# A two-layer MLP on one Trainium2 core: `x @ w_in` of three passes written as Strassen's seven half-size products

## The chip, the cores and the metric

The kernel runs on one core of a Trainium2 chip. Its engines are TensorE (PE; PEld is its weight load), VectorE (DVE), ScalarE (ACT), GpSimd (POOL) and SyncE (SP), which here only issues DMA transfers. The metric is the device time of one execution in microseconds (us); the median of three runs is given.

## The reference

An attention block produces `x` (2304 tokens by 512), and two MLP layers follow, each with `d_ff` = 2048:

```
x = attention(q, k, v)                      # 2304 x 512
h = x @ moe_w_in;   g = h * sigmoid(h);     x2  = g @ moe_w_out
h = x2 @ moe2_w_in; g = elu(h);             out = g @ moe2_w_out
```

All inputs are float64 or float32 and the result is float32. Weights come as float64 bit patterns and are decoded to float32 on the chip.

## The kernel before

Each matrix product is done in fp32r (32-bit matmul operands) with every operand split into a high and a low part; three of the four products of parts are kept: high x high, high x low, low x high. So one 128-wide contraction step costs three matmuls.

The MLP part has four passes: (layer, half of `d_ff`) = (0, 0), (0, 1), (1, 0), (1, 1). A pass holds the split weights of 8 slices `f` of 128 hidden units and runs over the tokens in blocks: nine blocks of 256 in the first pass, which runs beside the attention, and one block of 256 and four of 512 in each later pass. A unit is one block and one `f`. `g1` (L510) does `x @ w_in` of a unit: 4 contraction steps x 3 = 12 matmuls into a PSUM tile `ph`. ACT, DVE and POOL then make the activation and its split (`t`, `gh`, `gl`, L527 to L539; layer 0: tanh, add and multiply; layer 1: minimum, exp, add and maximum). `g2` (L574 for layer 0, L576 for layer 1), issued 3 units later (`LAG`), multiplies by `w_out` and sums over the 8 `f` in PSUM. In layer 0 the moving operand of `g2` is `g` (so a matmul is as wide as the token block), in layer 1 it is the weight (always 512 wide). The first half's sums go to DRAM (`yp`) and come back as `part` in the second half, where they are added (L591, L597).

The weights of the next pass are loaded (L139, L144, three staging buffers `ws`), decoded (`wf`: two ACT steps L158, L160 and three DVE steps L169, L170, L176) and split (`wh` on ACT L186, `wl` on POOL or DVE L188) a step at a time between the matmuls: `tick`, called four times in every `g1` and `g2`, takes one step of a list. Every engine executes its instructions in the order in which the program issues them; there is one SP queue for nearly all transfers. `x32` holds the attention's result, later `x2`, in SBUF for the whole run; `split_x` (L471, L474) splits it again for every block of every pass.

## Time and profile before

| quantity | value |
|---|---|
| three timed runs | 967.91, 968.86, 969.98 us (median 968.86) |
| profiled execution, first to last instruction (span) | 966.0 us |
| PE busy / DVE busy / ACT busy / POOL busy | 928.7 / 512.0 / 438.5 / 352.9 us |
| mean granted TensorE clock | 0.980 of full speed |

The page states only a span for the profiled execution and no total of its own; the median of the timed runs is 2.9 us above that span. Sums below are made against the span, and those 2.9 us are then put on top. The first 272 us hold the attention together with first-pass blocks, 272 to about 375 us the rest of the first pass, and the three later passes fill the time from about 375 us to 962 us. Since matmuls are pipelined and their ends are modelled, the busy time of PE says only that matmuls were in flight; the step between the starts of two matmuls is what one costs.

### The profile page before, as it was taken

What the parts mean: (1) busy time and instruction counts of PE and PEld (TensorE: products, weight loads), DVE (VectorE), ACT (ScalarE), POOL (GpSimd) and SP (SyncE); (2) the same over time, 40 slices, a digit from 0 to 9 for tenths busy, and PEclk for the clock granted to TensorE, in tenths of its full rate; (3) what the DMA queues carried; (4) which work ended last, traced back from release to release, by engine and by line L of the source; (5) the groups of instructions that cost most, each with busy time, mean ns of one, the idle gap of its engine ahead of it and who ended that gap; (6) DMA issues with size and microseconds to landing.
All of it is one profiled execution on the core that took longest, in us unless ns stands there. A gap on an engine that the chain in (4) does not pass through costs nothing.

```text
span 966.0 us, 16438 instructions
## 1 busy us (share of the span) xinstructions
PE 928.7 (96%) x6488; PEld 800.9 (83%) x6493; DVE 512.0 (53%) x841; ACT 438.5 (45%) x995; POOL 352.9 (37%) x363
## 2 busy tenths in 40 slices
PE   8388989999999999999999999999999999999998
PEld 5267879999999999888888887888888888888886
DVE  6677544444537857545453367656543544334232
ACT  4676545455446666443433445434333433222221
POOL 4577543553443354222223432222224422222221
PEclk9679999999999999999999999999999999999999
DMA  9944343233233632322121103122101011112021
GB/s 184 217 151 110 86 111 87 71 92 81 53 102 123 191 125 89 108 66 77 55 91 42 43 23 97 57 88 66 44 1 43 27 40 66 44 44 88 1 87 44
DMA packets 93485, 77.61 MB, mean 80 GB/s; under 512 B 61664, under 2 KB 82144, under 8 KB 92384
## 3 DMA queue, kind: packets, MB, share of 16 engines
q1 hardware_dynamic: 91008, 75.97, 26.9%
q8 instruction: 51, 0.84, 0.4%
q10 hardware_dynamic: 2400, 0.59, 0.3%
q14 instruction: 26, 0.21, 0.1%
HBM read 62.39 MB, written 14.16 MB: 79 GB/s over the span
## 4 chain that ended last, share of the span: by engine, by line
PE 62%; DVE 1%; ACT 1%; issue 0%; DMA 0%; SPq 0%; DVEq 0%; ACTq 0%
PE ph L510 31%; PE y L576 19%; PE y L574 12%; DMA ws<-in_moe_w_out_dram 0%; DVE part L597 0%; DVE xl L474 0%; DVE t L532 0%; ACT t L533 0%; ACT xh L471 0%; DVE wf L176 0%; DVE wf L169 0%; ACT gh L537 0%; DVE wf L170 0%; ACT ws L160 0%; ACT wf L158 0%
## 5 line engine op out<-in xcount | busy, mean ns | idle before, releaser
L539 POOL TENSOR_TENSOR gl<-t,gh 128x256 fp32r<-128x256 f32 (+1 forms) x192 | 204.5, 1066 | 526.2 <-ACT gh L537 472.8
L510 PE MATMUL ph<-xh,wh 128*128 128x256 f32 (+1 forms) x768 | 251.6, 340 | 4.7 <-DVE t L529 2.4
L510 PE MATMUL ph<-xl,wh 128*128 128x256 f32 (+1 forms) x768 | 250.4, 339 | 3.4 <-DVE xl L474 3.3
L510 PE MATMUL ph<-xh,wl 128*128 128x256 f32 (+1 forms) x768 | 177.9, 337 | 0.0
L510 PEld LDWEIGHTS ph<-xh,wh 128*128 128x128 f32 x768 | 145.6, 190 | 22.9 <-DVE t L529 3.0
L510 PEld LDWEIGHTS ph<-xl,wh 128*128 128x128 f32 x768 | 145.6, 190 | 21.2 <-DVE xl L474 5.0
L537 ACT CAST gh<-t 128x256 fp32r<-128x256 f32 (+1 forms) x192 | 98.8, 514 | 115.9 <-DVE t L529 63.4
L574 PE MATMUL y<-gh,wh 128*128 128x256 f32 (+1 forms) x448 | 145.3, 324 | 0.0
L510 PEld LDWEIGHTS ph<-xh,wl 128*128 128x128 f32 x768 | 127.9, 189 | 15.6 <-issue 0.6
L574 PE MATMUL y<-gl,wh 128*128 128x256 f32 (+1 forms) x448 | 140.6, 314 | 0.0
L574 PE MATMUL y<-gh,wl 128*128 128x256 f32 (+1 forms) x448 | 140.6, 314 | 0.0
L533 ACT ACTIVATE t<-t 128x512 f32<-128x512 f32 (+1 forms) x80 | 47.1, 589 | 195.8 <-DVE t L532 195.8
L529 DVE SCALAR_TENSOR_TENSOR t<-t,ph 128x256 f32<-128x256 f32 (+1 forms) x112 | 55.3, 494 | 143.6 <-ACT t L527 143.5
L532 DVE TENSOR_SCALAR t<-ph 128x512 f32<-128x512 f32 (+1 forms) x80 | 51.0, 637 | 122.3 <-PE ph L510 121.9
L576 PE MATMUL y<-wh,gh 128*128 128x512 f32 x288 | 112.2, 390 | 0.0
L576 PE MATMUL y<-wh,gl 128*128 128x512 f32 x288 | 112.2, 390 | 0.0
L576 PE MATMUL y<-wl,gh 128*128 128x512 f32 x288 | 112.0, 389 | 0.0
L527 ACT ACTIVATE t<-ph 128x256 f32<-128x256 f32 (+1 forms) x112 | 49.7, 444 | 121.9 <-PE ph L510 115.8
L474 DVE TENSOR_TENSOR xl<-x,xh 128x256 fp32r<-128x256 f32 (+1 forms) x96 | 68.4, 730 | 45.7 <-ACT xh L471 45.1
L574 PEld LDWEIGHTS y<-gh,wh 128*128 128x128 f32 x448 | 85.6, 191 | 7.4 <-issue 1.0
L574 PEld LDWEIGHTS y<-gl,wh 128*128 128x128 f32 x448 | 85.7, 191 | 5.0
L574 PEld LDWEIGHTS y<-gh,wl 128*128 128x128 f32 x448 | 85.5, 191 | 5.0
(90 smaller groups left out, 1207.8 us busy)
## 6 DMA issues: line engine op xcount, KB each, us to landing
ws<-in_moe_w_in_dram SPq DMA_DIRECT2D x32, 512.0 KB
ws<-in_moe_w_out_dram SPq DMA_DIRECT2D x32, 512.0 KB
rows<-in_v_dram SPq DMA_DIRECT2D x36, 144.0 KB
yp<-yo SPq DMA_DIRECT2D x10, 512.0 KB
part<-yp SPq DMA_DIRECT2D x10, 512.0 KB
out_dram<-part SPq DMA_DIRECT2D x18, 256.0 KB
yp<-yo SPq DMA_DIRECT2D x4, 1024.0 KB
part<-yp SPq DMA_DIRECT2D x4, 1024.0 KB
```

The source lines that it names most:

```text
L474: nc.vector.tensor_tensor(lo[c - 1], src[:, c - 1, :], hi[c - 1].bitcast(F32), ALU.subtract)
L510: nc.tensor.matmul(ph[:, :nb], a[:, c, :], b[c], start=m == 0, stop=m == 3 * KC - 1)
L527: nc.scalar.activation(t, h, AF.Tanh, scale=0.5)
L529: nc.vector.scalar_tensor_tensor(t, t, 1.0, h, op0=ALU.add, op1=ALU.mult)
L532: nc.vector.tensor_scalar_min(t, h, 0.0)
L533: nc.scalar.activation(t, t, AF.Exp)
L537: nc.scalar.copy(gh, t)
L539: nc.gpsimd.tensor_tensor(gl, t, gh.bitcast(F32), ALU.subtract)
L574: nc.tensor.matmul(y[d // share][:, h:h + nb], wm[:, sl], gm, start=first and d % share == 0, stop=last, skip_group_check=True)
L576: nc.tensor.matmul(y[d], gm[:, sl], wm, start=first, stop=last)
```

## The change

The first pass keeps its form (nine blocks of 256). In the three later passes the tokens are taken as three duos of 2 x 384 (768) tokens, and `x @ w_in` of a duo is done with Strassen's scheme (in Winograd's form): tokens, contraction (2 x 256) and hidden units (pairs of slices `f`, index `j` = 0 to 3) are each halved, and seven products of half-size blocks replace eight. A product is 4 `j` x 2 contraction steps x 3 = 24 matmuls, 384 wide (L944). Products 0, 2, 3 and 4 add up in one set of four PSUM banks, 1, 5 and 6 in the other. After products 0, 2 and 3 ACT copies the running sums out (L956); after 1, 5 and 6 DVE adds such a copy to a bank (L952). Only then does the next product of the set continue in the bank.

The half-size operands are sums: of weights (four DVE additions per pair, L761 to L767), and of `x` (four DVE additions of 128x768 per duo, L803). Each operand is split again (ACT cast L733; subtraction on DVE L736 or POOL L735). `g2` follows for each half of the duo: 8 slices, 384 wide in layer 0 (L1033), 512 wide in layer 1 (L1035). `x` no longer stays in SBUF: when the attention is done, four transfers write it to DRAM (`xd`), and each duo's part is loaded back (`xraw`); between the layers it goes through DRAM too (`x2`).

The work of ACT, DVE, POOL is no longer taken a step at a time. Each piece is a `Job` with an engine, an assumed duration, predecessors, an event of PE after which it may start, and a due time. `pump` is called after each product step (or quarter of a `g2` slice); it issues, among the jobs that could start before the planner's present time, the one with the earliest start, and of equals the one due first. `need` issues at once what the next matmuls depend on. Subtractions may go to POOL or DVE, whichever the planner expects to be done first; DVE jobs with `port=True` and all POOL jobs are planned one after the other.

On PE a stretch of the second layer reads so before: the last matmuls of a `g2` on the 512 hidden-side columns (`y`), then a `g1` unit of 12 (`ph`), then `g2` again.

```order
L576 MATMUL y_7509<-wh_7090,gh 128x512
L576 MATMUL y_7509<-wh_7090,gl 128x512
L576 MATMUL y_7509<-wl_7091,gh 128x512
L510 MATMUL ph<-xh,wh_6780 128x512
L510 MATMUL ph<-xl,wh_6780 128x512
L510 MATMUL ph<-xh,wh_6780 128x512
L510 MATMUL ph<-xl,wh_6780 128x512
L510 MATMUL ph<-xh,wh_6780 128x512
L510 MATMUL ph<-xl,wh_6780 128x512
```

Now the second layer has runs of product matmuls; here the end of product 1 and the start of product 2 (`wAA`, `wSS`: weight sums; `xhr`, `xlr`: split sums of `x`; `pc`: the banks).

```order
L944 MATMUL pc_8908<-xhr_5102,wAA3h_5091 128x384
L944 MATMUL pc_8908<-xlr_5103,wAA3h_5091 128x384
L944 MATMUL pc_8908<-xhr_5102,wAA3l_5092 128x384
L944 MATMUL pc_8836<-xhr_5412,wSS0h_5094 128x384
L944 MATMUL pc_8836<-xlr_5413,wSS0h_5094 128x384
L944 MATMUL pc_8836<-xhr_5412,wSS0l_5095 128x384
L944 MATMUL pc_8836<-xhr_5412,wSS0h_5094 128x384
L944 MATMUL pc_8836<-xlr_5413,wSS0h_5094 128x384
```

The alternation of `g1` and `g2` is gone: 28 such steps of six 384-wide matmuls stand together, then 16 slices of `g2`.

On ACT in the second layer the old order repeats exponentials (L533) and casts (L537) of units with steps of the decoder (`wf`, `ws`) and casts of `x` between them.

```order
L160 ACTIVATE ws_7392<-ws_7392 128x512
L533 ACTIVATE t_7587<-t_7587 128x512
L537 CAST gh_7588<-t_7587 128x512
L158 ACTIVATE wf_7606<-ws_7454 128x512
L160 ACTIVATE ws_7454<-ws_7454 128x512
L533 ACTIVATE t_7628<-t_7628 128x512
L537 CAST gh_7629<-t_7628 128x512
L471 CAST xh_7655<-x32_98 128x512
L471 CAST xh_7662<-x32_98 128x512
```

Now, between products 0 and 4 of the first duo of the last pass, the copies of the running sums (`hg` from `pc`, L956) stand in one queue with decoding (`raw`, `ws`), casts and activations.

```order
L704 ACTIVATE raw3_4396<-ws_8786 128x512
L705 ACTIVATE ws_8786<-ws_8786 128x512
L956 COPY hg0_4408<-pc_8836 128x384
L956 COPY hg1_4409<-pc_8846 128x384
L956 COPY hg2_4410<-pc_8855 128x384
L704 ACTIVATE raw4_4397<-ws_8794 128x512
L705 ACTIVATE ws_8794<-ws_8794 128x512
L956 COPY hg3_4411<-pc_8866 128x384
L733 CAST xhr_5100<-xt_4405 128x768
L841 ACTIVATE hg0_4408<-pc_8879 128x384
L733 CAST wh1_5536<-raw3_4396 128x512
L844 ACTIVATE hg0_4408<-hg0_4408 128x384
```

The copies of product 0 are queued around two decoder steps (`ws_8794`) that need a transfer to have landed; product 2 on those banks waits for each copy.

On DVE at the end of the first pass, after the attention, decoding is now mixed with the first sums of `x` and of weights (`xraw`: `x` loaded back from DRAM; `s1t`: a weight sum; `t`: activations of first-pass units).

```order
L762 TENSOR_TENSOR raw1_4394<-raw0_4393,raw1_4394 128x256
L516 SCALAR_TENSOR_TENSOR t_4600<-t_4600,ph_4585 128x256
L474 TENSOR_TENSOR xl_4617<-x32_98,xh_4610 128x256 x2
L717 SCALAR_TENSOR_TENSOR raw2_4395<-ws_4386,raw2_4395 128x512
L803 TENSOR_TENSOR xt_4405<-xraw3_4404,xraw1_4402 128x768
L516 SCALAR_TENSOR_TENSOR t_4646<-t_4646,ph_4630 128x256
L709 TENSOR_SCALAR raw3_4396<-raw3_4396 128x512
L803 TENSOR_TENSOR xraw1_4402<-xraw1_4402,xraw0_4401 128x768
```

Before, only decoder steps, `xl` and evictions stood between those activations (L529 then, L516 now); L803 waits for the transfers of `xraw`, and the next activation is queued behind it.

The diff, cut to its core:

```diff
-    WIDE = [(0, 2 * P)] + [(t_, 4 * P) for t_ in range(2 * P, NT, 4 * P)]
-    BLOCKS = {(0, 0): [(t_, 2 * P) for t_ in range(0, NT, 2 * P)], (0, 1): WIDE, (1, 0): WIDE, (1, 1): WIDE}
     NB0 = 2 * P
-    NBM = 4 * P
+    BLOCKS = [(t_, NB0) for t_ in range(0, NT, NB0)]
+    NB = 3 * P
+    NDUO = NT // (2 * NB)
+    PASSES = [(0, 1), (1, 0), (1, 1)]
...
+    ON_ACT = (0, 2, 3)
+    T_TICK, T_C, T_G = 0.52, 1.04, 2.08
+    PASS = NDUO * (7 * FP // 2 * T_C + 2 * FP * T_G)
...
-    def following(u):
-        layer, ps, n, _ = u
-        if n + 1 < len(BLOCKS[layer, ps]):
-            return layer, ps, n + 1
-        if ps + 1 < NPASS:
-            return layer, ps + 1, 0
-        return (layer + 1, 0, 0) if layer == 0 else None
-
-    ypart = {}
-
-    units = [
-        (layer, ps, n, f) for layer in range(2) for ps in range(NPASS)
-        for n in range(len(BLOCKS[layer, ps])) for f in range(FP)
-    ]
+    held = {}
+
+    units = [(n, f) for n in range(len(BLOCKS)) for f in range(FP)]
...
+    def keep_x(b):
+
+        xd[b] = dram.tile([P, KC, S], F32, tag=f"xd{b}", name=f"xd{b}")
+        nc.sync.dma_start(xd[b], x32[:, :, b * S:(b + 1) * S])
...
+        def start(self):
+
+            if self.gate is not None and self.gate not in events:
+                return None
+            t = events.get(self.gate, -1e9)
+            if self.port:
+                t = max(t, clock_of["port"])
+            for p in self.preds:
+                if p.end is None:
+                    return None
+                t = max(t, p.end)
...
+        def emit(self):
+            t = self.start()
+            assert t is not None
+            waiting.remove(self)
+            self.fn()
+            clock_of[self.eng] = t + self.dur
+            if self.port:
+                clock_of["port"] = t + self.dur
+            self.end = t + self.dur + self.lat
+
+    def pump(t):
+
+        while True:
+            best = None
+            for job in waiting:
+                s = job.start()
+                if s is not None and s < t and (best is None or (s, job.due) < best[:2]):
+                    best = (s, job.due, job)
+            if best is None:
+                return
+            best[2].emit()
...
+    ACT_ = {2 * P: 0.41, NB: 0.50, DM: 0.62, 2 * NB: 0.82}
+    VEC_ = {2 * P: 0.42, NB: 0.56, DM: 0.69, 2 * NB: 0.96}
+    GPS_ = {2 * P: 0.74, NB: 1.02, DM: 1.30, 2 * NB: 1.86}
...
+    def two_jobs(hi, lo, src, width, preds, gate, due):
+
+        a = Job("A", ACT_[width], lambda: nc.scalar.copy(hi(), src), preds, gate)
+        return Job(
+            "G", GPS_[width], lambda: nc.gpsimd.tensor_tensor(lo(), src, hi().bitcast(F32), ALU.subtract), [a], due=due,
+            other=("V", VEC_[width], lambda: nc.vector.tensor_tensor(lo(), src, hi().bitcast(F32), ALU.subtract)),
+        )
...
+            s0 = Job("V", VEC_[H], lambda s=s, o=o: sub(s, o[:, :H], o[:, H:], ALU.add), [do] + before.get(j - 2, []), port=True)
+            s1_ = Job("V", VEC_[H], lambda e=e, o=o: sub(o[:, :H], e[:, :H], o[:, :H], ALU.subtract), [s0, de], port=True)
+            aa = pair("AA", e, DM, [de], 0)
+            sa = pair("SA", o, DM, [s1_], 3 * NJ * T_C)
+            st = pair("S1", s, H, [s0], 5 * NJ * T_C)
+            m0 = Job("V", VEC_[H], lambda e=e, s=s: sub(e[:, :H], s, e[:, :H], ALU.subtract), [aa, s1_], port=True)
+            m1 = Job("V", VEC_[H], lambda e=e: sub(e[:, H:], e[:, H:], e[:, :H], ALU.subtract), [m0], port=True)
+            ss = pair("SS", e, DM, [m1], 2 * NJ * T_C)
+            before[j] = [st, m0]
...
+        got = x_loaded[number]
+        last = x_jobs.get((number - 1, 3))
+        t = vec(T, x22, x12, ALU.subtract, got, *([last] if last else []))
+        p0 = two(0, x11, got)
+        p1 = two(1, x21, got)
+        d = vec(x12, x12, x11, ALU.subtract, t)
+        n = vec(x11, T, x11, ALU.add, t, d, p0)
+        p2 = two(2, x11, n)
+        p3 = two(3, T, n)
+        m = vec(x11, x21, x11, ALU.subtract, p2)
+        p4 = two(4, x11, m)
+        p5 = two(5, x12, d)
+        p6 = two(6, x22, t)
...
+    banksets = [[(ps_d, "d"), (ps_d, "d"), (ps_h, "h"), (ps_h, "h")], [(ps_y, "y0"), (ps_y, "y1"), (ps_a, "a"), (ps_a, "a")]]
+    PRODUCTS = [("AA", 0), ("AA", 1), ("SS", 0), ("SA", 0), ("SA", 1), ("S1", 0), ("SS", 1)]
+    SETS = [0, 1, 0, 0, 0, 1, 1]
...
+                for j in range(NJ):
+                    t = need([weight_jobs[name, g, j], x_jobs[number, k]] + snap.get((k, j), []))
...
+                    now[0] = max(now[0], t)
+                    wh, wl = w1[name, j]
+                    o = half * 2 * P
+                    acc_ = bank[j][:, :NB]
+                    for c in range(2):
+                        cs = slice(o + c * P, o + (c + 1) * P)
+                        for m, (a, b) in enumerate(((wh, xh), (wh, xl), (wl, xh))):
+                            nc.tensor.matmul(
+                                acc_, a[:, cs], b[:, c, :], start=fresh and c == 0 and m == 0,
+                                stop=c == 1 and m == 2, skip_group_check=True,
+                            )
+                    now[0] += T_C
+                    gate = (number, k, j)
+                    events[gate] = now[0] + 0.15
+                    soon = now[0] + (NJ - 1) * T_C
+                    add = lambda out, x, y: Job("V", VEC_[NB], lambda: nc.vector.tensor_tensor(out, x, y, ALU.add), [], gate)
+                    if k in (0, 2, 3):
+                        dst = (part1, None, part2, part3)[k][j]
+                        after = {0: 2, 2: 3, 3: 4}[k]
+                        snap[after, j] = [Job("A", ACT_[NB], lambda dst=dst, acc_=acc_: nc.scalar.copy(dst, acc_), [], gate, due=soon)]
+                    elif k == 1:
+                        one_ = add(acc_, acc_, part1[j])
+                        one_.preds.extend(snap[2, j])
+                        act = activation_jobs(layer, part1[j], acc_, lambda j=j: part1[j], [one_], gate, soon + 10 * T_C, 0 in ON_ACT)
+                        free[use][j] = [act]
+                        split(j, part1[j], [act])
+                    elif k == 4:
+                        act = activation_jobs(
+                            layer, part1[j], acc_, lambda j=j: part1[j], [ready[j]], gate, GEMM2 + j * 0.5, 1 in ON_ACT
+                        )
+                        free[use][j] = [act]
+                        split(NJ + j, part1[j], [act])
+                    elif k == 5:
+                        one_ = add(part3[j], acc_, part3[j])
...
+                        snap[6, j] = [one_]
+                        act = activation_jobs(layer, part3[j], part3[j], own(j), [one_] + turn[-2:-1], None, 1e9, 3 in ON_ACT)
+                        turn.append(act)
+                        split(FP + NJ + j, part3[j], [act])
+                    else:
+                        one_ = add(acc_, acc_, part2[j])
+                        act = activation_jobs(layer, part2[j], acc_, lambda j=j: part2[j], [one_], gate, GEMM2 + FP * T_G + j * 0.5, 2 in ON_ACT)
+                        free[use][j] = [act]
+                        split(FP + j, part2[j], [act])
+                    pump(now[0])
+                    yield
+
...
+                for k in range(FP):
+                    m = h * FP + k
+                    t = need([weight_jobs["w2", g, k], ready[m]])
...
+                    for d in range(ny):
+                        for n_, (wm, gm) in enumerate(((wh, gh), (wh, gl), (wl, gh))):
+                            first, last_ = k == 0 and n_ == 0, k == FP - 1 and n_ == 2
+                            sl = slice(d * P, (d + 1) * P)
+                            if layer == 0:
+                                nc.tensor.matmul(y[d][:, :NB], wm[:, sl], gm, start=first, stop=last_)
+                            else:
+                                nc.tensor.matmul(y[d], gm[:, sl], wm, start=first, stop=last_)
+                        now[0] += T_G / ny
...
+                n, f = units[i]
...
+                    for b in range(B):
+                        keep_x(b)
+                    load_x(0, 0)
+                    now[0] = -TICKS * T_TICK * (len(units) + LAG - i)
...
+                    weights_first(0, 0.0, {
+                        "AA": lambda j: "wide", "S1": lambda j: "wide", "SA": lambda j: "rest",
+                        "SS": lambda j: "rest" if j == FP // 2 - 1 else "wide",
+                    })
+                    weights_second(0, 0.0, lambda k: "w2")
+                    x_work(0, 0.0, lambda k: "wide" if k < 2 else "rest" if k == 2 else (0, k - 3, FP // 2 - 1))
```

## Rows read from the trace of the kernel before

**Rows 1.** Page, part 1 and the clock row of part 2, whole span.

```profile
PE 928.7 (96%) x6488; PEld 800.9 (83%) x6493; DVE 512.0 (53%) x841; ACT 438.5 (45%) x995; POOL 352.9 (37%) x363
...
PEclk9679999999999999999999999999999999999999
```

**Rows 2.** Page, part 4: the chain that ended last, by line.

```profile
PE ph L510 31%; PE y L576 19%; PE y L574 12%; DMA ws<-in_moe_w_out_dram 0%; DVE part L597 0%; DVE xl L474 0%; DVE t L532 0%; ACT t L533 0%; ACT xh L471 0%; DVE wf L176 0%; DVE wf L169 0%; ACT gh L537 0%; DVE wf L170 0%; ACT ws L160 0%; ACT wf L158 0%
```

**Rows 3.** Windows, by stage: busy us (x instructions) per engine, PEclk, DMA share, GB/s.

```profile
272.00:375.00 103.00, 101.43 (x896) 99.17 (x895) 67.31 (x120) 65.31 (x154) 41.43 (x44) 1.00 0.39 124
...
400.00:580.00 180.00, 180.00 (x834) 150.65 (x833) 89.36 (x121) 71.24 (x127) 55.91 (x43) 1.00 0.20 62
580.00:780.00 200.00, 198.55 (x922) 165.36 (x921) 115.18 (x162) 85.20 (x153) 60.40 (x49) 1.00 0.16 56
780.00:962.00 182.00, 182.00 (x810) 150.75 (x808) 67.65 (x99) 49.60 (x82) 43.30 (x35) 1.00 0.12 44
```

**Rows 4.** Timeline of PE, last blocks of the first pass: start us, us, operation.

```profile
332.59 0.64 PE L510 MATMUL ph<-xh,wl 128*128 128x256 f32 x4
...
373.58 0.28 PE L510 MATMUL ph<-xh,wh 128*128 128x256 f32 x1
...
375.02 0.28 PE L574 MATMUL y<-gh,wh 128*128 128x256 f32 x1
```

**Rows 5.** Timeline of PE, 512-wide blocks of the second pass.

```profile
403.27 0.39 PE L574 MATMUL y<-gh,wh 128*128 128x512 f32 x1
...
405.99 0.39 PE L510 MATMUL ph<-xh,wh 128*128 128x512 f32 x1
```

**Rows 6.** Lines by form, PE: 512-wide matmuls | busy us, mean ns.

```profile
L510 PE MATMUL ph<-xl,wh 128*128 128x512 f32 x384 | 149.7, 390 | 0.4 <-DVE xl L474 0.4
...
L576 PE MATMUL y<-wh,gh 128*128 128x512 f32 x288 | 112.2, 390 | 0.0
...
L574 PE MATMUL y<-gh,wh 128*128 128x512 f32 x128 | 49.8, 389 | 0.0
```

**Rows 7.** Lines by form, other engines: x count | busy us, mean ns.

```profile
L539 POOL TENSOR_TENSOR gl<-t,gh 128x512 fp32r<-128x512 f32 x96 | 127.3, 1326 | 351.4 <-ACT gh L537 309.6 <-issue 41.8
...
L539 POOL TENSOR_TENSOR gl<-t,gh 128x256 fp32r<-128x256 f32 x96 | 77.3, 806 | 174.8 <-ACT gh L537 163.2 <-issue 5.9 <-PE y L574 5.6
...
L537 ACT CAST gh<-t 128x512 fp32r<-128x512 f32 x96 | 59.7, 622 | 68.0 <-DVE t L535 46.7 <-DVE t L529 21.3
...
L160 ACT ACTIVATE ws<-ws 128x512 uint32<-128x512 uint32 x64 | 42.5, 664 | 0.0
...
L537 ACT CAST gh<-t 128x256 fp32r<-128x256 f32 x96 | 39.0, 407 | 47.9 <-DVE t L529 42.0 <-DVE t L535 5.0 <-PE ph L510 0.5
...
L529 DVE SCALAR_TENSOR_TENSOR t<-t,ph 128x256 f32<-128x256 f32 x80 | 33.3, 416 | 67.3 <-ACT t L527 67.2
...
L529 DVE SCALAR_TENSOR_TENSOR t<-t,ph 128x512 f32<-128x512 f32 x32 | 22.0, 688 | 76.4 <-ACT t L527 76.4
L169 DVE TENSOR_SCALAR wf<-wf 128x512 f32<-128x512 f32 x48 | 21.8, 453 | 0.2 <-ACT wf L158 0.2
```

**Rows 8.** Timeline of ACT: first step after an accumulation group of matmuls.

```profile
333.33 0.39 ACT L527 ACTIVATE t<-ph 128x256 f32<-128x256 f32 x1
```

**Rows 9.** Windows of 4 us: the first three loads of second-pass weights.

```profile
276.00:280.00 4.00, 4.00 (x51) 3.61 (x50) 2.03 (x6) 2.16 (x5) 0.97 (x1) 1.00 0.91 313
```

**Rows 10.** Timeline of DVE: two-input SBUF operations alone and beside a POOL one.

```profile
397.58 1.67 DVE L176 SCALAR_TENSOR_TENSOR wf<-ws,wf 128x512 int32<-128x512 int32 x1
...
604.47 0.68 DVE L474 TENSOR_TENSOR xl<-x,xh 128x512 fp32r<-128x512 f32 x1
```

**Rows 11.** Timeline of POOL over the same time as the DVE row at 397.58.

```profile
397.23 1.48 POOL L539 TENSOR_TENSOR gl<-t,gh 128x512 fp32r<-128x512 f32 x1 [2.90 <-ACT gh L537]
```

**Rows 12.** Timeline of PE at the third pass's start: a wait of the matmuls.

```profile
586.17 0.50 PE L510 MATMUL ph<-xh,wh 128*128 128x512 f32 x1 [1.03 <-DVE t L535]
```

558 lines of the change are left out of this document (407 added, 151 removed).

## Prediction

> **What bounds the kernel now.** I read the page first: PE has matmuls in flight for 96% of the span and the granted clock, after an early dip, stands at 9 tenths or more [rows 1]. The chain that ended last runs along PE: 62% of the span in three matmul lines, and every other line rounds to 0% [rows 2]. The windows by stage show where this holds. From 400 to 962 us PE is without work for 1.45 us (198.55 of 200) and nowhere else, at clock 1.00, while DVE, ACT and POOL are busy 272, 206 and 160 of 562 us, which is 48%, 37% and 28% [rows 3]. So in the three later passes the price of the time is the number of matmuls times the step between their starts, and nothing else.
>
> The steps come from the timeline of PE. Twelve 256-wide matmuls start 1.44 us apart in all (373.58 to 375.02), 0.120 us each [rows 4]; twelve 512-wide ones 2.72 us (403.27 to 405.99), 0.2267 us each [rows 5]. Twice the columns cost 0.1067 us more, so a line through both has a fixed 0.0133 us per matmul. Read so, 384 columns cost 0.0133 + 1.5 x 0.1067 = 0.1733 us.
>
> **The change, part by part.** *Matmuls removed and added.* Before, the three passes hold 512-wide matmuls in nine groups (three products each of L510, L576, L574): 3 x (384 + 288 + 128) = 2400 [rows 6], 544.0 us at 0.2267. The 256-wide block of each pass adds 3 x 96 in `g1` and 96 in the `g2` of layer 0, 384 in all, by the loops: 46.1 us. Sum 590.1 us. After, nine duos have 7 x 24 = 168 product matmuls each, 1512; `g2` of layer 0 has 3 duos x 2 x 8 x 12 = 576, all 384 wide: 2088 x 0.1733 = 361.9 us. `g2` of layer 1 stays 512 wide: 6 duos x 2 x 8 x 9 = 864, 195.8 us. Sum 557.8 us, 32.3 less. The saving consists of two parts: one product in eight gone (216 matmuls of 384, 37.4 us), and narrower tiles, which pay the fixed part more often (5.1 us back).
>
> The trace has no 384-wide matmul. From below its price is three quarters of a 512-wide one, 0.170; from above one and a half 256-wide ones, 0.180. That is -7 or +14 us on 2088 matmuls. I take the line, since both neighbours show the same fixed part.
>
> The Trainium skill, TensorE: Matmul & The Clock Gate, section Back-to-back issue gap, gives the isolated gap as columns by 2.4 GHz plus 2.5 ns. With it the 512-wide step would be 0.2158 and the 256-wide 0.1092, both about 0.011 shorter than the trace shows [rows 4, 5]; as an estimate from that page the saving would be 34 us. The trace decides, and it makes narrow tiles dearer than the page does.
>
> *Sums, copies and splits* are added on DVE and ACT. Durations at 384 lie halfway between 256 and 512: DVE with PSUM (416 + 688) / 2 = 0.55 us, ACT (407 + 622) / 2 = 0.51, POOL (806 + 1326) / 2 = 1.07; going on by the same slope, 768 costs DVE 0.95, ACT 0.84 and POOL 1.85; decoder steps 0.66 on ACT and 0.45 on DVE [rows 7]. The order gives the counts. From the first product sum to the last eviction DVE has 693 instructions: 406 at 384, 84 at 768, 130 at 512, 37 at 256 (0.42) and 36 of 0.45: 424 us beside 553 us of PE, 77% where it was 48%. ACT has 669 (468 at 384, 60 at 768, 57 at 512, 8 at 256, 76 decoder steps): 239 + 50 + 35 + 3 + 50 = 377 us, 68%. POOL keeps 73 subtractions, 88 us. The heaviest duos on DVE are the third and the sixth, where the next weights are made as well: 97 and 95 instructions, 57 us each, beside 62 us of PE. So all of it fits beside the matmuls, and I cost it at nothing as long as no engine is late where PE waits.
>
> *Where PE waits.* Product 2 starts on a bank when ACT has copied it; products 3 and 4 likewise, and product 6 after a DVE sum. A product has four steps of 6 x 0.1733 = 1.04 us on four banks, so between the end of a step and the next on the same bank lie three steps, 3.1 us. What must fit: the start of ACT after the last matmul, the copy of 0.51 us, and the way back. In the trace the last four 256-wide matmuls of a unit end at 332.59 + 0.64 = 333.23 [rows 4], and ACT starts on their bank at 333.33 [rows 8]: 0.1 us. 0.7 us of 3.1, so 2.4 us is what the queue ahead may take. Queued ahead of the last copy of product 0 are two decoder steps, 1.3 us, if their transfer has landed. It fits; these waits cost 0, and 0 to 2.4 us more of delay stay covered.
>
> *The end of the first pass.* The planner's tick stands for 0.52 us, but four quarter units of 3 x 0.120 us make 0.36. So the jobs there are issued as though there were 1.4 times as long as there is; what is late is the queue, not the matmuls. Per unit (24 x 0.120 = 2.88 us) DVE gets up to 3.9 us of instructions around the first sums of `x`, then 3 us on average in the last block. The old kernel ran this stage with DVE at 67.3, ACT at 65.3 and POOL at 41.4 of 103 us and lost 103 - 101.4 = 1.6 us on PE [rows 3]; a unit's activation is not needed for three units, 8.6 us. The four transfers of `x32` (4.7 MB) and the 1.6 MB back take 15 + 5 = 20 us at the 313 GB/s that the weight loads reached here [rows 9], with the sum of `x` (L803) and then a unit's activation waiting in DVE's queue. If they land 5 us late, the three units hide it. Ends: 0, and 10 us if the whole way back is late; I take 1.
>
> *Port.* Two-input DVE operations from SBUF took 0.68 us alone and 1.67 us beside a POOL subtraction of 1.48 [rows 10, 11]; there are more of them now, but fewer POOL ones. The Trainium skill, SBUF — State Buffer, section Who interferes with whom, says that in this pair whoever comes first blocks the other for the whole instruction. These rows agree. All 88 us of POOL, spread evenly, would put 9.8 us on the DVE queue of each duo; only the third and the sixth then overflow (57 + 9.8 against 62 us, 5 us each). So 0 to 10 us, and I take 2, since those two duos are the only ones where it can show.
>
> Waits at the turn of passes before (1.03 us at 586 [rows 12]) may stay or go; I leave them. The sum: 966.0 - 32.3 + 1 + 2 = 936.7 us of span, plus the 2.9 us by which the median of the runs lies above the span: **939.6 us**, 3.0% less.
>
> **The rivals.** *A: the end as forecast*, PE nearly gapless: 936 (no waits at all) to 945.
>
> *B: DVE becomes the bound in heavy duos.* For it speaks 77% on average, 92% in two duos, and in-order queues whose ACT steps it waits for; against it, that rows 3 show DVE, ACT and POOL together at 1.7 times the time with PE losing only 1.6%. If every port collision costs its whole length and the end of the first pass loses 10 us: 936.6 + 20 = 957.
>
> *C: slower, by the handing over of banks.* Place: products 2, 3, 4 and 6 of each duo, 36 hand-overs. Mechanism: one ACT or DVE step ahead of the copy waits for something that is late (a weight transfer, another engine's step), and the copies behind it wait too, while PE stands. A hand-over that is 2.4 us late costs nothing; past that every microsecond is lost, and when 36 of them lose 32.3 / 36 = 0.9 us each, that is when each is 3.3 us late, the gain is gone. At 1.4 us each, the time is 936.6 + 50 = 987. Against it: ACT is at 68% and few of its steps wait for transfers.
>
> *D: 384-wide matmuls cost like one and a half 256-wide ones*: 939.6 + 14 = 953.5. Against it is the equal fixed part of rows 4 and 5.
>
> *E: nothing gained.* PE does the fewer products, but each duo loses 3.6 us at its turns, where products start on sums and banks of the last one: 969. No row speaks for it; the order has the next duo's operands queued half a duo ahead.
>
> **How the numbers follow.** Chances: A 0.68, B 0.14, D 0.05, C 0.09, E 0.04. Predicted 939.6, from A. The range takes A with 2 us below it (no waits, and a part of the cheaper end of the 384-wide price) and B with D nearly whole: 934 to 957; C and E, 0.13, are left out, and some of B's tail. A change within 0.2% (2 us) can't be told from none. Faster: A, B, D, 0.87; same: E, 0.04; slower: C, 0.09.
>
> **What would show it.** Right: in the windows of the later passes PE without idle time, steps of 2.08 us per twelve 384-wide matmuls, DVE near 77%, ACT near 68%, and a stage of 558 us or a few more. Wrong, by B: idle time of PE put down to DVE in the third and sixth duo. By C: PE waiting for ACT's `hg` copies at products 2 to 4, and ACT idle before decoder steps on transfers. By D: steps of 2.16 us. At the end of the first pass: DVE idle for `xraw`, and PE waiting for `gh` or `gl`. The prediction fails if PE's idle time after 375 us is over 20 us, or the step of a 384-wide matmul is not 0.173 us.

## The result, and the profile after

The changed kernel took **936.13 us** (median of 4 runs, 935.54 to 937.35) beside 968.38 us of the kernel before (4 runs, 966.89 to 969.98): a ratio of 0.968, interval 0.9655 to 0.9707. The forecast was 939.6. The profiled execution took 935.57 us with a span of 933.8 us, where the span before was 966.0.

The page after, lines that answer to [rows 1], and below it the chain that ended last, which answers to [rows 2]:

```profile
PE 897.7 (96%) x6656; PEld 830.8 (89%) x6661; DVE 627.2 (67%) x1132; ACT 537.1 (58%) x1247; POOL 263.2 (28%) x292
...
PEclk9679999999999999999999999999999999999999
...
PE pc L944 28%; PE pc L1035 21%; PE pc L1033 11%; PE y L542 2%; PE ph L498 1%; DVE t L516 0%; DVE raw L713 0%; DVE raw L767 0%; DVE part L997 0%; DVE raw L766 0%; DVE xlr L736 0%; DVE s1t L761 0%; DVE raw L717 0%; ACT t L513 0%; DVE wAA3l L736 0%
```

PE is still the bound and holds the chain in three matmul lines: the products (L944) and the two forms of `g2` (L1033, 384 wide, layer 0; L1035, 512 wide, layer 1). New in the list are the first pass's own lines at its end (L542, L498, and behind them L516 on DVE). The windows by stage of the kernel after, which answer to [rows 3], show both halves of the story:

```profile
272.00:375.00 103.00, 99.00 (x853) 96.58 (x852) 65.97 (x121) 55.20 (x133) 30.86 (x35) 0.98 0.45 150
400.00:580.00 180.00, 180.00 (x1040) 180.00 (x1039) 142.65 (x241) 103.50 (x204) 35.75 (x27) 1.00 0.37 119
580.00:760.00 180.00, 180.00 (x907) 163.03 (x906) 138.50 (x242) 117.52 (x239) 29.48 (x24) 1.00 0.28 94
760.00:930.00 170.00, 169.97 (x847) 152.66 (x845) 102.73 (x178) 85.55 (x175) 14.98 (x12) 1.00 0.19 65
```

In the three later passes PE has no gap at all (529.97 of 530 us), although DVE is busy 79% in one of the windows. At the end of the first pass it is the other way round: PE lost 4.0 of 103 us, where it had lost 1.6, and the clock is 0.98 there.

The new step, in the timeline of PE in the changed kernel (start us, us, operation), which answers to [rows 4, 5]:

```profile
375.83 0.33 PE L944 MATMUL pc<-xhr,wAA0h 128*128 128x384 f32 x1
...
377.91 0.33 PE L944 MATMUL pc<-xhr,wAA2h 128*128 128x384 f32 x1
```

Twelve 384-wide matmuls start 2.08 us apart in all, 0.1733 us each, as the line through 256 and 512 columns had it. The other new shapes, from the lines by form (x count | busy us, mean ns of one | idle before), which answer to [rows 7]:

```profile
L736 DVE TENSOR_TENSOR xlr<-xraw,xhr 128x768 fp32r<-128x768 f32 x47 | 46.3, 985 | 13.0 <-ACT xhr L733 12.9
L733 ACT CAST xhr<-xraw 128x768 fp32r<-128x768 f32 x54 | 44.7, 834 | 6.0 <-DVE xraw L803 5.0 <-PE pc L944 0.7
...
L952 DVE TENSOR_TENSOR pc<-pc,hg 128x384 f32<-128x384 f32 x54 | 30.1, 561 | 24.9 <-PE pc L944 24.6
L956 ACT COPY hg<-pc 128x384 f32<-128x384 f32 x54 | 25.9, 479 | 65.2 <-PE pc L944 64.3
```

0.561 us for a sum was 0.55 in the forecast, 0.479 for a copy 0.51, 0.985 and 0.834 at 768 were 0.95 and 0.84.

**Where the time went.** Two marks cut the spans. In the kernel before, the last matmul of the first pass's last `g2` is followed by the next one at 373.58 [rows 4], with three `g1` units of the next pass (36 matmuls, 4.32 us) done ahead of it; in the kernel after the same point is at 374.78, with three steps of the first product (18 matmuls, 3.12 us) done ahead of it. Without this work of the next pass the first pass is over at 369.26 and at 371.66: 2.4 us later. From there to the end it is 596.7 and 562.1 us: 34.6 less. The matmuls were to give 32.3 of these; the 2.3 that remain are two waits at the third pass's start, at 586.17 [rows 12] and 588.10, of which the trace before shows 1.45 us as idle [rows 3] and the rest lies in late starts beside them. The trace after has no such wait.

The 2.4 us are not all due to the change. The part up to the end of the attention is shared, and it takes a few microseconds more or less from run to run (298.96 to 304.16 us up to the start of the 21st last `g1` unit of the first pass, over all runs below). The timeline of PE, first in the kernel before, then after: the attention's last matmuls, that unit's first one, and in the kernel after the mark at 374.78:

```profile
287.23 1.38 PE L443 MATMUL pso<-aT,vw 64*64 64x60 f32 x40
...
301.59 0.28 PE L510 MATMUL ph<-xh,wh 128*128 128x256 f32 x1
```

```profile
285.61 1.38 PE L438 MATMUL pso<-aT,vw 64*64 64x60 f32 x40
...
299.98 0.28 PE L498 MATMUL ph<-xh,wh 128*128 128x256 f32 x1
...
374.78 0.34 PE L944 MATMUL pc<-xhr,wAA3h 128*128 128x384 f32 x1
```

The shared part was 1.6 us shorter in the run after. From that unit on, the first pass takes 67.7 us before and 71.7 after: 4.0 us is what the change costs there. To the end of the span it is 664.4 and 633.8 us, 30.6 less, and that is the change's own share of the 32.2 us between the two spans.

### The profile page after: what moved, and what is told of

It is laid out like the page before. It is cut to its first block, busy times and chain, and to the rows that moved or that the text cites. A ratio compares the mean times of both kernels' runs of the same rounds, so it can differ in the third digit from the quotient of the medians.

```text
span 933.8 us, 17299 instructions
## 1 busy us (share of the span) xinstructions
PE 897.7 (96%) x6656; PEld 830.8 (89%) x6661; DVE 627.2 (67%) x1132; ACT 537.1 (58%) x1247; POOL 263.2 (28%) x292
## 4 chain that ended last, share of the span: by engine, by line
PE 63%; DVE 2%; ACT 1%; issue 0%; ACTq 0%; DVEq 0%
PE pc L944 28%; PE pc L1035 21%; PE pc L1033 11%; PE y L542 2%; PE ph L498 1%; DVE t L516 0%; DVE raw L713 0%; DVE raw L767 0%; DVE part L997 0%; DVE raw L766 0%; DVE xlr L736 0%; DVE s1t L761 0%; DVE raw L717 0%; ACT t L513 0%; DVE wAA3l L736 0%
## 5 line engine op out<-in xcount | busy, mean ns | idle before, releaser
L542 PE MATMUL y<-gh,wh 128*128 128x256 f32 x288 | 86.9, 302 | 0.0
L498 PE MATMUL ph<-xh,wh 128*128 128x256 f32 x288 | 77.9, 295 | 6.2 <-DVE t L516 5.1
L542 PE MATMUL y<-gh,wl 128*128 128x256 f32 x288 | 82.1, 285 | 0.0
L542 PE MATMUL y<-gl,wh 128*128 128x256 f32 x288 | 82.1, 285 | 0.0
L498 PE MATMUL ph<-xl,wh 128*128 128x256 f32 x288 | 76.2, 289 | 2.9 <-DVE xl L474 2.8
L516 DVE SCALAR_TENSOR_TENSOR t<-t,ph 128x256 f32<-128x256 f32 x72 | 30.0, 416 | 68.0 <-ACT t L513 67.9
L1035 PE MATMUL pc<-wl,grw 128*128 128x512 f32 x192 | 74.8, 389 | 0.0
L1035 PE MATMUL pc<-wh,glk 128*128 128x512 f32 x192 | 74.8, 389 | 0.0
L1035 PE MATMUL pc<-wh,ghk 128*128 128x512 f32 x192 | 74.7, 389 | 0.0
L1035 PE MATMUL pc<-wh,grw 128*128 128x512 f32 x192 | 74.7, 389 | 0.0
L944 PE MATMUL pc<-xhr,wSA 128*128 128x384 f32 x288 | 74.5, 334 | 0.0
L956 ACT COPY hg<-pc 128x384 f32<-128x384 f32 x54 | 25.9, 479 | 65.2 <-PE pc L944 64.3
L498 PEld LDWEIGHTS ph<-xh,wh 128*128 128x128 f32 x288 | 55.2, 192 | 8.6 <-DVE t L516 6.3
L498 PEld LDWEIGHTS ph<-xl,wh 128*128 128x128 f32 x288 | 55.2, 192 | 4.4 <-DVE xl L474 3.7
L542 PEld LDWEIGHTS y<-gh,wh 128*128 128x128 f32 x288 | 56.0, 194 | 2.2 <-issue 1.0
L519 ACT CAST gh<-t 128x256 fp32r<-128x256 f32 x72 | 29.3, 407 | 49.4 <-DVE t L516 49.3
L542 PEld LDWEIGHTS y<-gl,wh 128*128 128x128 f32 x288 | 56.0, 194 | 0.0
L542 PEld LDWEIGHTS y<-gh,wl 128*128 128x128 f32 x288 | 55.8, 194 | 0.0
L736 DVE TENSOR_TENSOR xlr<-xraw,xhr 128x768 fp32r<-128x768 f32 x47 | 46.3, 985 | 13.0 <-ACT xhr L733 12.9
```

The costliest lines, as they stand in the source:

```text
L498: nc.tensor.matmul(ph[:, :nb], a[:, c, :], b[c], start=m == 0, stop=m == 3 * KC - 1)
L516: nc.vector.scalar_tensor_tensor(t, t, 1.0, h, op0=ALU.add, op1=ALU.mult)
L519: nc.scalar.copy(gh, t)
L542: nc.tensor.matmul(y[d // 2][:, h:h + nb], wm[:, sl], gm, start=f == 0 and m == 0 and d % 2 == 0, stop=f == FP - 1 and m == 2, skip_group_ ...
L736: other=("V", VEC_[width], lambda: nc.vector.tensor_tensor(lo(), src, hi().bitcast(F32), ALU.subtract)),
L944: nc.tensor.matmul(acc_, a[:, cs], b[:, c, :], start=fresh and c == 0 and m == 0, stop=c == 1 and m == 2, skip_group_check=True,)
```

## The experiments

What the chip's runs differ in lies on either side of one instant, the first matmul of the first product. Ahead of it, runs differ by up to 5 us that arise in the first 200 us, in code that all these kernels share; from it to the end the changed kernel repeats within 0.1 us. The table gives both from the profiled runs, with the median of the timed ones. The column "from the unit" counts from the start of the 21st last `g1` unit of the first pass to the end, without the shared part; it is 664.4 us in the kernel before, and the changed kernel repeats there within 0.2 us. The runs of the kernel before that stand beside them had medians of 966.3 to 966.7 us.

| kernel | from the unit, us | first product, us | from there to the end, us | median us | ratio to before (interval) |
|---|---|---|---|---|---|
| changed kernel | 633.8 | 367.36 | 566.4 | 936.13 | 0.968 (0.966 to 0.971) |
| the same again | 633.9 | 370.55 | 566.4 | 936.57 | 0.969 (0.967 to 0.972) |
| product 0 twice | 671.2 | 366.57 | 603.9 | 973.74 | 1.008 (1.006 to 1.011) |
| tick 0.44 | 627.7 | 362.60 | 566.4 | 931.71 | 0.965 (0.962 to 0.967) |
| tick 0.36 | 627.3 | 359.81 | 566.4 | 929.37 | 0.962 (0.959 to 0.965) |
| tick 0.30 | 629.7 | 364.64 | 569.3 | 934.17 | 0.966 (0.963 to 0.968) |
| four banks | 631.9 | 366.25 | 567.2 | 935.75 | 0.968 (0.965 to 0.971) |
| tick 0.36, four banks | 627.3 | 362.51 | 566.4 | 930.73 | 0.963 (0.960 to 0.966) |
| one more DVE operation per sum | 633.9 | 367.38 | 566.4 | 936.22 | 0.969 (0.966 to 0.972) |
| two more | 648.0 | 367.69 | 580.6 | 950.60 | 0.983 (0.979 to 0.986) |
| three more | 684.0 | 366.33 | 618.1 | 986.84 | 1.020 (1.017 to 1.024) |
| one more ACT copy per hand-over | 633.8 | 368.81 | 566.4 | 938.28 | 0.970 (0.966 to 0.974) |
| no POOL in the later passes | 632.8 | 368.82 | 566.4 | 937.00 | 0.969 (0.966 to 0.972) |

### Is it the eighth product?

```diff
-                    for c in range(2):
+                    for c in [0, 1] * (2 if k == 0 else 1):
```

Expected: 

> Product 0 of every duo issues its 24 matmuls twice (the first half of the pass over the bank is thrown away by the second, which starts the bank anew), so that PE has eight products' worth of matmuls; the order of all other engines stays as it is. Theory (the later passes cost what their matmuls cost): 9 duos x 24 x 0.1733 us = +37.4 us, so 973.5 us, about 5 us above the kernel before, which is the price of the narrower tiles. Rival (other engines or the turns set the time there, and the saved matmuls only uncovered them): part of the 37.4 us is swallowed, 936 to 965 us.

Measured: 973.74 us, and from the first product on 603.87 us in place of 566.43: 37.4 us more, which is 216 x 0.1733. Nothing of the added matmuls was swallowed, so PE alone sets the time of the later passes. With eight products' worth of matmuls the new kernel takes 0.8% longer than the old one (1.008, 1.006 to 1.011), by its narrower tiles and the end of its first pass.

### What the end of the first pass waits for

In the changed kernel, PE's waits between 272 and 420 us (us in total, times, longest):

```profile
PE ph L498 <- DVE t L516: 2.7, 4, 1.2
PE ph L498 <- ACT xh L468: 1.1, 1, 1.1
```

The worst spot, engine by engine, from the timeline of the changed kernel (in brackets the idle time before the row and what ended it); first DVE, then ACT, then PE:

```profile
313.38 0.69 DVE L713 SCALAR_TENSOR_TENSOR raw<-raw,ws 128x512 int32<-128x512 int32 x1
314.10 0.69 DVE L717 SCALAR_TENSOR_TENSOR raw<-ws,raw 128x512 int32<-128x512 int32 x1
314.71 0.41 DVE L516 SCALAR_TENSOR_TENSOR t<-t,ph 128x256 f32<-128x256 f32 x1
...
315.16 0.41 ACT L519 CAST gh<-t 128x256 fp32r<-128x256 f32 x1 [2.16 <-DVE t L516]
315.47 0.66 ACT L704 ACTIVATE raw<-ws 128x512 f32<-128x512 f32 x1
316.03 0.64 ACT L705 ACTIVATE ws<-ws 128x512 uint32<-128x512 uint32 x1
316.58 0.70 ACT L468 CAST xh<-x 128x256 fp32r<-128x256 f32 x2
...
315.18 0.39 PE L498 MATMUL ph<-xh,wh 128*128 128x256 f32 x1 [0.64 <-DVE t L516]
317.02 0.38 PE L498 MATMUL ph<-xh,wh 128*128 128x256 f32 x1 [1.10 <-ACT xh L468]
```

It reads backwards from the last row. PE at 317.02 waits for the split of `x` on ACT at 316.58. ACT had been idle for 2.16 us, not for want of work: at the head of its queue stood the copy L519, which needs DVE's L516, and behind it two decoder steps and then the split. DVE had L516 at 314.71, behind decoder steps and sums. One late instruction on DVE thus holds PE twice, once by the bank that L516 frees (0.64 us) and once across ACT's queue (1.10 us). The windows of 16 us around it, in the kernel before and in the changed one (PE, PEld, DVE, ACT, POOL):

```profile
300.00:316.00 16.00, 16.00 (x136) 16.00 (x135) 11.54 (x21) 9.57 (x22) 4.65 (x6) 1.00 0.52 173
```

```profile
300.00:316.00 16.00, 15.27 (x126) 14.87 (x124) 14.52 (x27) 8.22 (x19) 4.68 (x5) 1.00 0.61 201
```

DVE's busy time is 14.5 of 16 us there, 3 us more than before. Two edits go at the two ends of this: what the planner puts in, and how soon PE needs L516 back.

```diff
-    T_TICK, T_C, T_G = 0.52, 1.04, 2.08
+    T_TICK, T_C, T_G = 0.36, 1.04, 2.08
```

Expected: 

> The planner's tick at the end of the first pass stands for 0.36 us, what three 256-wide matmuls take, and not 0.52 us. Theory (the planner believes that it has 1.4 times the time, so it puts too much into DVE's queue per unit and the first pass's own step at L516 comes late): the 4.0 us that PE lost between 272 and 375 us fall to 1 to 2 us, 933 to 935 us. Rival (DVE has this work to do in any case, and what is put off here is late for the first products of the first duo): 936 us or up to 940, with the gap after 375 us.

```diff
+    hbanks = [(ps_h, "h")]
...
-        ph = ps_h.tile([P, 512], F32, tag="h", name="ph")
+        pool, tag = hbanks[0]
+        hbanks.append(hbanks.pop(0))
+        ph = pool.tile([P, 512], F32, tag=tag, name="ph")
...
                     attn_pools.close()
...
+                    hbanks.append((ps_d, "d"))
```

Expected: 

> From the end of the attention on, the sums of g1 alternate between the two banks of pool h and the two of pool d, four in place of two. Theory (the waits of PE on L516 come from there being two banks: a unit's L516 must be done within one and a half units, not three): the waits on L516 of 2.7 us go, one on the split of x (1.1 us) stays, 933 to 934.5 us. Rival (DVE is simply late, and g2 then waits for the same steps three units on): the same waits appear at g2, 935.5 to 937 us.

Both edits together: 

> Both edits at once: tick 0.36 us and four banks. Theory: PE loses 1 us or less between 272 and 375 us, 932 to 933.5 us, under both kernels. Rival (one limit behind both, DVE's work in that stage): no better than the better of the two alone.

Measured: the tick brought 929.37 us, more than expected, and PE's waits between 272 and 420 us fell from 3.8 us on these two lines to none; the product starts at 359.81 where it started at 367.36 (1.0 us of this arises earlier in the run). Four banks alone brought nothing that the medians can tell apart (935.75); from the 21st last unit on, where the changed kernel repeats within 0.2 us, they gained 1.9 us of the 6.5 that the tick gained. There the waits on L516 went as the theory had it (the last 14 units before the product run 2.88 us apart without a gap), but the wait across ACT grew and another came in, as the waits of that kernel show (L469 and L947 are L468 and L944 of the changed one):

```profile
PE ph L501 <- ACT xh L469: 2.0, 1, 2.0
PE pc L947 <- DVE yo L556: 0.5, 1, 0.5
```

Both edits together (930.73) were no better than the tick alone. So the two banks are where PE felt most of it, and the cause is that the planner filled DVE's queue for time that wasn't there: taking that away takes all of the waits away, while more banks only move them.

The gain is larger than the waits, and the spacing of the units in the trace says why. From the 17th last to the last unit of `g1` are 16 x 2.88 = 46.1 us of matmuls; the changed kernel took 52.9, the one with the tick 46.5. Of the 6.8 us lost, 3.8 are the waits shown as idle (the 0.64 and 1.10 above and three of 0.23 to 1.23 later). The unit at 315.18, in which the long one falls, took 6.2 us instead of 2.9, and windows of 1 us in the changed kernel (PE, granted clock, DMA share, GB/s) show the rest of it:

```profile
316.00:317.00 1.00, 0.00 (x0) 1.00 0.77 202
317.00:318.00 1.00, 0.90 (x4) 0.85 0.73 266
318.00:319.00 1.00, 1.00 (x6) 0.50 0.08 33
319.00:320.00 1.00, 1.00 (x7) 0.50 0.00 0
320.00:321.00 1.00, 1.00 (x7) 0.50 0.00 0
321.00:323.00 2.00, 2.00 (x18) 0.97 0.83 229
```

After the waits the granted clock stands at 0.50, that is 1.2 of 2.4 GHz, for a little over 3 us, in which PE's matmuls start 0.21 us apart in place of 0.12: with the edges (0.85 and 0.97) 1.7 us of work. The Trainium skill, TensorE: Matmul & The Clock Gate, section A second HAM failure mode: psum-queue depth-cycling, tells of a kernel that cycles through PSUM banks, in which PE idles briefly between groups of matmuls so often that the clock goes to and fro between its two levels. The trace here shows one such fall behind brief waits, and with the tick at 0.36 the clock stays at 1.00 here.

The waits don't bring the clock down every time. The run with three more DVE operations (below) has the same first pass and the same two waits, 0.65 and 1.10 us, and in it the clock stays (windows of PE, that run first, then the changed kernel):

```profile
316.00:320.00 4.00, 2.82 (x21) 1.00 0.45 134
```

```profile
316.00:320.00 4.00, 2.90 (x13) 0.71 0.39 125
```

The unit took 4.8 us there in place of 6.2, so the fall of the clock cost about 1.4 us. The other 1.6 of the 6.8 us lie in late starts at the five restarts, about 0.3 us each.

Two more ticks, with the changed kernel beside them as their measure:

The changed kernel again: 

> The changed kernel itself beside the runs of the other ticks, as their measure: 936 us, its first product at 366 to 368 us of the span and 566.4 us from there to the end.

Tick 0.44: 

> The tick at 0.44 us, halfway between 0.52 and 0.36. Theory (what DVE's queue gets per unit follows the tick): the waits of PE on L516 and L468 shrink with it, 930 to 934 us. Rival (it is one chance position of the split of x behind the decoder steps, which any other order would undo): 929.5 us, as with 0.36.

Tick 0.30: 

> The tick at 0.30 us, under the 0.36 us that three matmuls take. Theory (nothing is left to gain in the first pass, where PE waited 0.4 us with 0.36): 929 to 930 us, the 566.4 us behind the first product unchanged. Rival (the steps that the planner now puts off are late for the first duo): PE waits behind the first product, 931 to 940 us.

Measured: 936.57, 931.71 and 934.17 us. With 0.44 the first-pass waits were gone as well, and of the 2.8 us by which its span is longer than with 0.36, 2.4 lie ahead of the 21st last unit of `g1` (301.32 there, 298.96 with 0.36), in shared code; so 0.36 and 0.44 can't be told apart, and "the waits shrink with the tick" falls: they go at once. With 0.30 the rival held: the jobs that are put off come too late for the first duo, whose `g2` waits for its weights:

```profile
PE pc L1033 <- DVE wl L736: 1.9, 2, 1.5
```

and the time from the first product on is 569.3 us. Of the four values, 0.36 and 0.44 do equally well; 0.36 is what PE takes for three matmuls of 0.120 us, and a longer or a shorter tick (0.52, 0.30) loses, each at another place. The version with 0.36 beats both kernels: 0.962 of the kernel before (0.9588 to 0.9652), some 7 us under the changed one, of which 6.5 lie behind the shared part.

### How much cover the matmuls give

Three kernels put n = 1, 2 or 3 further operations behind each sum (the allocation of the spare tile is left out here):

```diff
-                    add = lambda out, x, y: Job("V", VEC_[NB], lambda: nc.vector.tensor_tensor(out, x, y, ALU.add), [], gate)
+                    def more(out, x, y):
+                        nc.vector.tensor_tensor(out, x, y, ALU.add)
+                        for _ in range(n):
+                            nc.vector.tensor_scalar_min(spare[0], out[:, :2 * P], 0.0)
+
+                    add = lambda out, x, y: Job("V", VEC_[NB], lambda: more(out, x, y), [], gate)
```

Two: 

> Behind each of the 108 sums that DVE adds in products 1, 5 and 6, two more DVE operations of 256 columns (0.41 us each) into a spare tile, in the same place of the queue. DVE then has 413 + 89 = 502 of the 562 us of the nine duos, 89%, and in the third and the sixth duo 52.7 + 9.8 = 62.5 and 50.7 + 9.8 = 60.5 us beside 62 us of PE. Theory (the work beside the matmuls is free until a duo's sum is over the duo's matmuls, since queues run half a duo ahead): 936 us plus 0 to 3. Rival B of the prediction (in-order queues jam well below 100%): PE waits for DVE in the heavy duos, 10 us or more, 946 us and up.

Three: 

> The same with three more operations each: DVE 546 of 562 us, 97%, and in the first, third and sixth duo 54.4 + 14.7 = 69 of 66.7, 67.4 of 62.4, 65.4 of 61.7 us. Theory: those duos overflow by 2.4 + 5.0 + 3.7 = 11 us, part of which the lighter duos behind them take up: 940 to 950 us. Rival B: 30 us or more, the jam spreading over all duos, 966 us and up.

Measured: 14.2 us more from the first product on with two, 51.6 with three. My sum over a duo failed (0 to 3, and 11); rival B's numbers held, but not its place, the heavy duos. PE's waits from 290 us on, with two more operations (the edit moves lines: L945, L954 and L962 are the products, their sum and the copy, before L944, L952 and L956):

```profile
PE pc L945 <- DVE hgw L954: 4.6, 10, 1.0
PE pc L945 <- ACT hg L962: 2.8, 4, 1.6
```

and with three:

```profile
PE pc L945 <- ACT hg L962: 14.5, 9, 4.3
PE pc L945 <- DVE hgw L954: 12.9, 17, 1.7
```

They come in light duos as well as in heavy ones, so it isn't the duo's sum that overflows. With two operations all ten waits on L954 stand in product 6, and each of the nine duos has one at the product's last step, on the last sum of product 5; the four on L962 stand at the first two steps of product 3. The timeline of DVE in the untouched changed kernel, at product 5 of the sixth duo (703.32 to 707.48 us on PE), shows what does:

```profile
704.56 0.56 DVE L952 TENSOR_TENSOR hgx<-pc,hgx 128x384 f32<-128x384 f32 x1 [0.41 <-PE pc L944]
705.04 0.55 DVE L843 TENSOR_SCALAR hg<-pc 128x384 f32<-128x384 f32 x1
705.60 0.56 DVE L952 TENSOR_TENSOR hgx<-pc,hgx 128x384 f32<-128x384 f32 x1
706.08 0.54 DVE L845 SCALAR_TENSOR_TENSOR hg<-hg,pc 128x384 f32<-128x384 f32 x1
706.64 0.56 DVE L952 TENSOR_TENSOR hgw<-pc,hgw 128x384 f32<-128x384 f32 x1
707.12 0.54 DVE L845 SCALAR_TENSOR_TENSOR hg<-hg,pc 128x384 f32<-128x384 f32 x1
707.68 0.56 DVE L952 TENSOR_TENSOR hgw<-pc,hgw 128x384 f32<-128x384 f32 x1
```

Sum and activation alternate, two operations in each 1.04 us of PE: in this stretch DVE has no idle time left, in a duo in which it is busy 82% on the whole. The last sum is done at 708.2, and PE's step of product 6 on that bank starts at 710.60. That is the slack, 2.4 us, the size that the prediction had for the hand-over. Seven of the nine duos have it at this place; the first and the third have 2.0 and 1.4. This gave a forecast for one operation more:

One: 

> One more DVE operation of 256 columns behind each of the 108 sums. New theory after two and three of them (the slack counts at each hand-over, not over a duo): in product 5 DVE already has two operations of 0.55 us in each step of 1.04 us, and the sum for a bank is done 2.4 us before product 6 needs it; four operations more make the last sum 1.4 to 1.6 us later, under 2.4, so nothing is lost: 566.4 to 567.5 us from the first product to the end, 936 to 938 us. By the same count two cost 2.8 to 3.3 us, 0.4 to 0.9 over, in each of nine duos. Rival (the loss is that of DVE's total load): a third of what three cost or half of what two cost, 7 us or more, 943 us.

Measured: 566.4 us, nothing lost, and 936.22 us in all; a loss in proportion to DVE's total load would have been 7 us. At the same product 5 the last sum is now done at 709.8 us, 1.6 later, with 0.8 of the 2.4 us left, where the step of product 6 starts at 710.62; the least that is left in any duo is 0.35 us, in the first. With two operations the last step of product 6 starts 0.05 us behind the end of its sum in each of the nine duos. So the slack at the hand-over says where the loss begins.

How large the loss then is, it doesn't say. By this count two operations are 0.4 to 0.9 us over per duo, and a duo lost 1.6 us on average (14.2 / 9); three would be 1.8 to 2.4 over, and a duo lost 5.7. Two things that the count leaves out are in the traces. ACT's copies wait for DVE in turn (the lines on L962). And the added operations of product 5 meet POOL: a row of theirs is 0.29 us long alone, but with two per sum 23 of these 72 rows are 0.39 to 1.9 us long, each beside a POOL subtraction, 15 us more in all. No run separates the two.

A wait shown as idle is not all that is lost here. With two operations more, the starts of PE's matmuls are late by some 14 us in all; 7.4 are shown as idle, and some 4 lie in about 50 starts that come late, but before the modelled end of the matmul ahead, so that the profile counts PE as busy.

The same for ACT, at the hand-over by copies (L956):

```diff
+                    def more(dst, acc_):
+                        nc.scalar.copy(spare[0], acc_[:, :2 * P])
+                        nc.scalar.copy(dst, acc_)
...
-                        snap[after, j] = [Job("A", ACT_[NB], lambda dst=dst, acc_=acc_: nc.scalar.copy(dst, acc_), [], gate, due=soon)]
+                        snap[after, j] = [Job("A", ACT_[NB], lambda dst=dst, acc_=acc_: more(dst, acc_), [], gate, due=soon)]
```

Expected: 

> Ahead of each of the 108 copies by which ACT hands the banks of products 0, 2 and 3 over, one more ACT copy of 256 columns (0.41 us) into a spare tile. ACT goes from 335 to 379 of 562 us, 67%. Theory (2.4 us of slack at each hand-over): four copies of 0.9 us in place of 0.5 fit in a product's 4.16 us, the last of them 1.6 us later than it was; nothing is lost, 936 us plus 0 to 2. Rival C of the prediction (the copies already come just in time behind the activations and splits): each hand-over of products 2 and 3 is late by up to the 1.6 us of its four copies, 18 times, 29 us: 950 to 965 us.

Measured: 566.4 us from the first product on, no wait of PE there. ACT is busy 357.5 of the first 562 us from the product on, where it was 334.6: 0.21 us for each of the 108 copies, half of what the expectation put in, so rival C's place has at least 0.8 us of room (four copies) and the run says no more. In the run with three DVE operations it does show, as the 14.5 us on L962: ACT's copies stand behind steps that wait for DVE. The mechanism exists, at another load.

Last, the port: all subtractions of the later passes go to DVE.

```diff
         return Job(
-            "G", GPS_[width], lambda: nc.gpsimd.tensor_tensor(lo(), src, hi().bitcast(F32), ALU.subtract), [a], due=due,
-            other=("V", VEC_[width], lambda: nc.vector.tensor_tensor(lo(), src, hi().bitcast(F32), ALU.subtract)),
+            "V", VEC_[width], lambda: nc.vector.tensor_tensor(lo(), src, hi().bitcast(F32), ALU.subtract), [a], due=due, port=True,
         )
```

Expected: 

> All subtractions of the later passes on DVE (the planner isn't given POOL as a choice), so that no POOL instruction meets DVE at the port there. DVE takes on the 89 us of POOL at about half the time, 46 us: 459 of 562 us, 82%. Theory (port and DVE's share are both covered after 375 us): from the first product of the first duo to the end 566.4 us as in the changed kernel; in the last units of the first pass DVE has more to do, so 936 to 940 us. Rival (the 2 us that I put down to the port are there, in DVE's queue): 934 us.

Measured: 566.4 us from the first product on, 937.00 in all: the collisions at the port cost nothing on PE's path, and neither does DVE without POOL's help. The surprise is DVE's own time: it took on all but one of 70 subtractions and is busy 430.5 of the first 562 us from the product on, where it was 412.6. That is 18 us more in place of the 46 counted. The rows of the 69 subtractions are 43.6 us long; against that, those of DVE's other operations, kind by kind, are 19.9 us shorter in sum than beside POOL, and operations overlap by 5.9 us more. So the collisions are real, as [rows 10, 11] had them, some 20 us in these passes, but DVE has the time.

## Why the prediction was right, and where not

- **Matmuls, -32.3 us: right.** The step of 0.1733 was met, the price of a product is shown by doubling one (37.4 us), and PE has no gap from 375 us on. Rival D falls with it, and E with the windows.
- **DVE and ACT beside the matmuls at no cost: right, by a criterion that is wrong.** The windows of the nine duos of the changed kernel, the third one and the sum:

```profile
496.50:558.90 62.40, 62.40 (x362) 62.40 (x361) 52.65 (x91) 40.54 (x80) 16.44 (x13) 1.00 0.27 89
...
sum 562.20, PE 562.20 PEld 528.29 DVE 412.80 ACT 334.59 POOL 88.98; mean PE 62.47 PEld 58.70 DVE 45.87 ACT 37.18 POOL 9.89
```

  DVE 73% (77% forecast), ACT 60% (68%), POOL 89 us (88); the third duo 52.7 us (57). The counts were too high since durations were added, while an operation starts before the last has ended (0.56 us each at 0.48 apart in the rows of product 5). "Only the third and the sixth then overflow" was the failing step: the cover ends where product 5's sums fall 2.4 us behind (1.4 in the third duo), in any duo, and two small operations more per sum are enough. That the sum over a duo gave the right zero here was luck as far as the criterion goes; one operation more still gave it, two didn't.
- **The hand-over of banks, 2.4 us for the queue: right.** The trace has 2.4 us at product 6 in seven of nine duos, and the tests of DVE put the edge there: with one more operation per sum 0.35 us or more is left, with two PE waits. Rival C didn't come. At ACT's copies the edge itself wasn't reached; the test shows 0.8 us of room.
- **The end of the first pass, +1: too small, and a second step that failed.** "A unit's activation is not needed for three units, 8.6 us" holds for `g2`, which reads it, but L516 also frees one of two banks, and the unit after the next starts on that. The time allowed is one and a half units (the unit's own `g2`, then the next unit with its `g2`, 36 matmuls or 4.3 us), not three; past it PE stood. The text had seen the planner's 1.4 times and drew the consequence for transfers only, which landed in time (the sum of `x` at L803 never waited for them). Measured from the end of the attention, the first pass took 4.0 us more than before (2.4 with the shared part, which happened to be 1.6 us shorter); against the kernel with the right tick it lost 6.4.
- **Port, +2: not there.** The run without POOL gives the same 566.4 us; the 20 us or so that the port took from DVE were covered.
- **Waits at the turns of passes, left: they went,** for 2.3 us. I had no row to take them away by.
- **The sum.** -32.3 for the matmuls, -2.3 for the turns, +4.0 for the first pass and -1.6 for the shared part make -32.2, the 966.0 - 933.8 of the two spans. The forecast of the span was 936.7; of its 2.9 us too much, 2.0 are the port, 2.3 the turns and 1.6 the shared part, and the first pass took back 3.0. The last 0.6 us of the 3.5 to the median are the offset, which was 2.9 us and is 936.13 - 933.8 = 2.3. So the large term was right by its mechanism, and that the small ones came out so close was luck: a term three microseconds too small stood against two that were two too large.

## What to carry to other kernels

When work is put beside matmuls, count it between the instant a bank is full and the instant PE needs it again, step by step and with the other steps in the same in-order queues; an engine that is busy 73% over a stage may have no idle time at that place. Where a buffer has two readers or a second use, take the earliest of its needs, not the one the data flow names. A planner whose unit of time is longer than the engine's can lose more than the waits it causes, since waits can take the clock with them: check that number against the trace first. And when two runs are compared by stage, count from a mark behind the part that they share, so that its spread isn't put down to the change.
